# Long convolution and two MLPs on one core: operand blocks of a token pair as separate tasks, a spent input place turned into tiles, and weight sums streamed for both batches

## The chip, the cores and the metric

The kernel runs on one core of one Trainium2 chip. The metric is the device time of one execution in microseconds. Of the kernel before there are three timed runs (1117.55, 1117.56 and 1119.34 us) and one execution taken by the hardware profiler.

## The reference

Input `x` has 2 batches of 3008 tokens with 256 features. Three layers follow each other:

```
X = rfft(x, axis=1);  y = irfft(X * (filt_r + 1j*filt_i), n=3008, axis=1)    # long convolution along tokens
h = y @ w_in (256 x 2048);  g = max(h,0) + alpha*min(h,0);  z = g @ w_out (2048 x 256)      # first MLP, m = 0
h = max(z @ w_in2, 0);  out = (h*h) @ w_out2                                          # second MLP, m = 1
```

All is float32. The kernel keeps the precision by writing a float32 operand as a high half (rounded to the matmul's format) and a low half (what is left): a product is then three matmuls, high by high, high by low, low by high.

## The kernel before, in words

Features lie on the 128 partitions in two halves d = 0, 1, tokens along the free axis. `XS[b]` holds batch b's activations, 2 halves of 3008 tokens; each layer's result is written over its input there. The 3008 tokens of a batch are six tiles: four of 512 and two of 480 (`TILES`). The 2048 hidden features are 16 slices f of 128.

The work has these stages in time:

1. The convolution of batch 0, a four-step Fourier transform by matmuls (class `Conv`, `c0`).
2. The direct stage: the first MLP of batch 0, tile by tile (`h_mm`, `h_act`, `g_split`, `o_mm`). Beside it run the preparation of all weights (`weights`: halves made, written to DRAM as `WD`), the weight sums of MLP 1 (`sums`, written to DRAM as `SD`), and the beginning of batch 1's convolution (`c1`).
3. Nine token pairs, in this order: MLP 1 of batch 0, MLP 0 of batch 1, MLP 1 of batch 1, each with three pairs of tiles g = 0, 2, 4 (`pairs`, names (m, b, g)). In a pair the product of the input layer is done for two tiles and two feature slices at once with seven products in place of eight (Strassen's scheme in Winograd's form). One such step is a `square` (line 766); a pair has eight, c = 0 to 7, one for each two slices f. A square issues 7 products of 3 matmuls (line 801) and, in between, 8 waiting halves of the output layer (`o_half`, lines 636 to 638, 3 matmuls each). The rest of batch 1's convolution runs in the first three pairs (lines 306 to 308, 406).

For its seven products a pair needs seven operand blocks of the tokens: 11, 21, 22 (pieces of `XS`), and the differences T1 = 12 - 11, T2 = 22 - T1, T3 = 22 - 12, T4 = 21 - T2. `blocks` (line 663) makes them. Each takes a slot from `xb` (8 slots during the first three pairs, 11 later) for high and low half: ACT copies with rounding (line 694), then DVE subtracts for the low half (line 696). A difference is one DVE instruction (line 679) into a tile of `tf`. The squares use them in the order 11, 21, T2, T3, T1, 22, T4; a block's slot comes free after its last use in square 7 of its pair. In the kernel before, all seven blocks of a pair are one task, whose steps follow each other: a copy waits for the low half of the block before, and T3's and T4's differences come right before their copies.

For its products a square needs sums of weight blocks S1, S2, S3 (384 columns, high and low). For batch 0 they are loaded from `SD` into two `ring` tiles, two squares ahead (`fetch_sums`, line 532). For batch 1 six of the eight are loaded once per MLP into a place of their own, `sums`, which takes the place of `XS[0]`, and the last two into the ring.

`tf` (9 tiles of 512 columns, float32) holds intermediate values, and results on their way out (line 648); `tr` (9 tiles, rounded format) holds the halves of hidden activations.

The order is computed when the program is built. `Order` keeps a list of tasks (generators) and a time for each engine. Each step of a task names the engines it can run on with a cost, the events it needs and the tiles it takes. `run` picks the step that could begin earliest, less the task's `lead`, and issues it there; a tile is taken when the plan says it will be free. TensorE's own order is written out in the loops, and the other engines are filled up to a little ahead of it. On the chip every engine works off its queue in order, and waits where the plan was too early. SP issues all DMAs, in one queue.

Of the kernel before, what the change touches and what calls it, by code (L numbers as in the profile page):

```python
# [11 lines left out]
F32R = mybir.dt.float32r  # L12
# [6 lines left out]
B, S, D, FF = 2, 3008, 256, 2048  # L19
# [4 lines left out]
NF = FF // 128  # L24
TILES = [(i * 512, 512) for i in range(4)] + [(2048, 480), (2528, 480)]
# [7 lines left out]
N_TF = 9  # L33
# [8 lines left out]
PE_HOOK = 0.7  # L42
# [3 lines left out]
V2 = 4.8  # L46
# [9 lines left out]
ADD_V = 1.1  # L56
AHEAD = 2.5

LEAD0 = 0.3
LOWS, SUBS, LOWW = "VG", "VG", "VG"  # L60
LEAD1 = 0.5
GATE = ("SD", 1, 7)
SLACK = 0.6
LATE = ("WD", 1, 10)

TINY = 2.0 ** -15
INF = float("inf")
# [7 lines left out]
class Free:  # L75
# [5 lines left out]
    def when(self, n):  # L81
        return self.t[n - 1][0] if len(self.t) >= n + self.keep else None
# [19 lines left out]
HURRY = {}, [], []  # L102


class Spare:
# [5 lines left out]
    def when(self, n):  # L111
        t = self.free.t
        return t[n - 1][0] if len(t) >= n + self.keep else None


class Order:
# [76 lines left out]
def conv_mlp_mlp(ctx, tc, x, fil, wts, alp, cst, out):  # L193
    nc = tc.nc
    V, A, G, T, SP = nc.vector, nc.scalar, nc.gpsimd, nc.tensor, nc.sync
# [5 lines left out]
    def sb(name, cols, dt=F32, place=None):  # L201

        return pool.tile([128, cols], dt, name=name, tag=place or name)

    XS = [sb("X0", 2 * S), sb("X1", S + UC)]
# [3 lines left out]
    ring = [sb(f"ring{i}", 768, F32R) for i in range(2)]  # L209
    places = {f"stg{i}": sb(f"stg{i}", 1024) for i in range(N_STG)}  # L210
    stg = Free(places.values())
    tf = Free(sb(f"tf{i}", 512) for i in range(N_TF))
    tr = Free(sb(f"tr{i}", 512, F32R) for i in range(N_TR))
    xin = [sb(f"xin{i}", 2048) for i in range(NXS)]
    xs = Free([])
# [11 lines left out]


    SD = [[dram.tile([2, 128, 384], F32, name=f"s{m}_{c}") for c in range(NF // 2)] for m in range(2)]
    SX = []  # L230
    spare = Spare(tf, KEEP_S)
    wx = Free([])
    bf, br, wf, wr = Spare(tf, 0), Spare(tr, 0), Spare(tf, 0), Spare(tr, 0)
    xb = Free([])
# [7 lines left out]
    class Conv:  # L242
# [4 lines left out]
        def __init__(self, b, bank, whole, us, xin):  # L247
            self.b, self.bank, self.whole, self.us, self.xin = b, bank, whole, us, xin
            self.x, self.f = {}, {}
# [275 lines left out]
        mark(("SD", m, c), end)  # L525

    def sx(b, c, k):
        if b == 0 or c >= 6:
            return ring[c % 2][:, k * 384:k * 384 + 384]
        return SX[0][:, c * 768 + k * 384:c * 768 + k * 384 + 384]  # L530

    def fetch_sums(m, b, g, c, after):
        for k in range(2):
            _, end = yield {"S": 0.6}, [("SD", m, c), *after], []
            if b and c < 6 and not SX:
                SX.append(sb("sums", 768 * 6, F32R, "X0"))
            SP.dma_start(f32v(sx(b, c, k)), SD[m][c][k])
            end = od.moved(end, 128 * 1536)
        mark(("S", m, b, g, c), end)
# [123 lines left out]
    def blocks(m, b, g):  # L663

        o, n = TILES[g]
        need = [("Y", b, g), ("Y", b, g + 1)]
        if m == 0:
            need = [("X", 1, h, u) for h in range(2) for u in range(o // 376, (o + 2 * n - 1) // 376 + 1)]
        k = pairs.index((m, b, g))
        if k:  # L670
            need.append(("xb", *pairs[k - 1], "T4"))
        x = {f"{d + 1}{j + 1}": XS[b][:, d * S + o + j * n:d * S + o + j * n + n] for d in range(2) for j in range(2)}
        own = {}

        def less(name, p, q):
            _, end = yield {"V2": 0.69}, need, [(spare, 1)]
            own[name] = tf.take()
            x[name] = own[name][:, :n]
            V.tensor_sub(x[name], x[p], x[q])

        for name in ("11", "21", "T2", "T3", "T1", "22", "T4"):
            if name == "T2":
                yield from less("T1", "12", "11")
                yield from less("T2", "22", "T1")
            elif name == "T3":

                yield HURRY
                yield from less("T3", "22", "12")
            elif name == "T4":
                yield from less("T4", "21", "T2")  # L690
                tf.give(od.free["V"], own["T2"])
            _, end = yield {"A": 0.6}, need, [(xb, 1)]
            t = xb.take()
            A.copy(t[:, :n], x[name])  # L694
            _, end = yield {"V2": 0.69}, [], []
            V.tensor_sub(t[:, 512:512 + n], x[name], f32v(t[:, :n]))  # L696
            if name in own and name != "T2":
                tf.give(end, own[name])
            xsp[m, b, g, name] = t
            mark(("xb", m, b, g, name), end)  # L700

    oq = []
    pb = Free([])
# [62 lines left out]
    def square(m, b, g, c):  # L766

        n, f0, f1 = TILES[g][1], 2 * c, 2 * c + 1
        d0, d1 = slice(0, 128), slice(128, 256)
        w = {"11": (WH[f0][:, d0], WL[f0][:, d0]), "12": (WH[f0][:, d1], WL[f0][:, d1]), "22": (WH[f1][:, d1], WL[f1][:, d1])}  # L770
        w["S4"] = WH[f1][:, d0], WL[f1][:, d0]
        operands = {1: ("11", "11"), 2: ("12", "21"), 3: ("S4", "22"), 4: ("22", "T4"), 5: ("S1", "T1"), 6: ("S2", "T2"), 7: ("S3", "T3")}
        ps = {}
        od.add(chain(m, b, g, c, ps), joined(m, b, g, c, ps), lead=1.0)
        waits = {6: [("US", m, b, g, c, 1)], 5: [("US", m, b, g, c, 6)], 3: [("US", m, b, g, c, 5)], 4: [("J", m, b, g, c)]}
        for k in (1, 2, 0, 6, 0, 7, 5, 0, 0, 3, 0, 4, 0, 0, 0):
            if k:
                a, x = operands[k]
                need = [("xb", m, b, g, x), ("W", m, b, f0), ("W", m, b, f1), ("S", m, b, 0 if b else g, c)]
                if not all(e in at for e in need):  # L780
                    od.run(always, need)
                until = od.free["T"]
                after = waits.get(k, [])
                while not (all(e in at for e in after) if after else pb.t):
                    until += 0.5
                    od.run(dict.fromkeys(od.free, until))
                first = not after
                if first:
                    began = pb.t[0][0]
                    ps[k] = pb.take()  # L790
                else:
                    ps[k] = ps[7 if k == 4 else 1]
                    began = 0.0
                od.free["T"] = max(od.free["T"], began, *(at[e] for e in need + after)) + 3 * (n + 32) / 2400
                bank = ps[k]
                if a in ("S1", "S2", "S3"):
                    r = int(a[1]) * 128
                    w[a] = tuple(sx(b, c, j)[:, r - 128:r] for j in range(2))
                (wh, wl), t = w[a], xsp[m, b, g, x]
                for j, (p, r) in enumerate(((wh, t[:, :n]), (wh, t[:, 512:512 + n]), (wl, t[:, :n]))):  # L800
                    T.matmul(bank[:, :n], p, r, start=(first and j == 0), stop=(j == 2), skip_group_check=True)  # L801
                mark(("P", m, b, g, c, k), od.free["T"] + LATENCY)
                if c == NF // 2 - 1:
                    xb.give(od.free["T"], xsp.pop((m, b, g, x)))
            elif oq:
                ready, args = oq.pop(0)
                od.free["T"] = max(od.free["T"], ready)
                o_half(*args)
            ahead = od.free["T"] + AHEAD_S
            od.run({"A": ahead, "V": ahead, "G": ahead + 0.6, "S": od.free["T"] + 2.6, **({} if b else {"T": od.free["T"] + PE_HOOK})})  # L810
        mark(("done", m, b, g, c), od.free["T"])
# [21 lines left out]
    with tc.manual_schedule():  # L833
# [72 lines left out]

        od.add(reclaim([("O", 0, 0, t5 - 1, 2)], 2), *(reclaim_xs() for _ in range(NXS)), lead=1.0)
        od.add(reclaim([("SD", m, c) for m in range(2) for c in range(NF // 2)] + [("U", 1, u) for u in range(NU)], N_STG - 2))
        od.add(*(blocks(*k) for k in pairs), lead=0.9)
        whole = [("X", 1, h, g) for h in range(2) for g in range(8)]  # L910
        for m, b in ((1, 0), (0, 1), (1, 1)):
            for f in range(NF):
                after = [("O", 1 - m, b if m else 0, t, f) for t in (t5 - 1, t5)]
                od.add(fetch(m, b, f, after))
                if b and f % 2:
                    od.add(fetch_sums(m, b, 0, f // 2, after + whole + [("done", *pairs[2], f // 2), ("xb", *pairs[2], "T4")]))
        flat = [(g, c) for g in range(0, len(TILES), 2) for c in range(NF // 2)]
        for i, (g, c) in enumerate(flat):
            od.add(fetch_sums(1, 0, g, c, [("done", 1, 0, *flat[i - 2])] if i > 1 else [("O", 0, 0, t5, 4)]), lead=1.0)

        now = max(od.free["T"], at["xs", 0, 0, 0])
        for i in range(len(seq)):
# [18 lines left out]
        spare.keep = 2  # L941
        for k in pairs:
            if k == (0, 1, 0):
                od.run(always, whole)
                pb.give(od.free["T"], c0.bank.take(), c0.bank.take())
            for c in range(NF // 2):
                square(*k, c)
# [82 lines left out]
```

## Time and profile before

| | |
|---|---|
| timed runs, median of 3 | 1117.56 us |
| the profiled execution, its own time | 1120.31 us |
| its span in the profile | 1118.5 us |
| granted clock, mean | 0.996 |
| PE busy | 1103.3 us |
| DVE, ACT, POOL busy | 839.2, 742.0, 118.3 us |
| moved by DMA | 110.67 MB |

The span runs from the first to the last instruction of the profile. PE is TensorE's matmul row; matmuls overlap, so the time between two starts, not the length of one, is what a matmul costs. A bracket behind a row says how long the engine stood idle before it and which instruction released it.

### The profile page before, as it was taken

How to read it: one execution, taken by the hardware profiler on the slowest of the kernel's cores; microseconds unless marked ns; L12 is line 12 of the kernel's file. 1: busy time of each engine (PE TensorE's matmuls, PEld its weight loads, DVE VectorE, ACT ScalarE, POOL GpSimd, SP SyncE). 2: the span in 40 equal slices, each digit the busy share in tenths (PEclk: the TensorE clock that was granted, in tenths of full speed). 3: DMA queues.
4: the chain of work that ended last, by engine and by line, in shares of the span. 5: the costliest groups of instructions: out<-in, count | busy, mean ns of one | idle time of the engine just before them, and what ended most of it. 6: DMA issues, size and time to landing. Idle time of an engine off the chain costs nothing.

```text
span 1118.5 us, 14481 instructions
## 1 busy us (share of the span) xinstructions
PE 1103.3 (99%) x4945; PEld 907.3 (81%) x4946; DVE 839.2 (75%) x1361; ACT 742.0 (66%) x1360; POOL 118.3 (11%) x111
## 2 busy tenths in 40 slices
PE   9999999999999998999899999999999999999998
PEld 4678888888888887888698888888888888888887
DVE  4888878888889687769885887977977756656554
ACT  4777575665677676666566866766766666766665
POOL 5600000100022323313210000000000000000000
PEclk9999999999999999999999999999999999999999
DMA  9655223225746323223478700000144200100100
GB/s 232 173 199 197 80 90 125 90 88 163 234 132 214 125 70 109 85 71 90 123 245 259 228 1 1 1 1 1 37 140 151 88 1 1 38 1 1 39 1 36
DMA packets 64634, 110.67 MB, mean 99 GB/s; under 512 B 7472, under 2 KB 36400, under 8 KB 64560
## 3 DMA queue, kind: packets, MB, share of 16 engines
q1 hardware_dynamic: 64560, 109.74, 31.2%
q8 instruction: 39, 0.64, 0.2%
q14 instruction: 35, 0.29, 0.1%
HBM read 79.43 MB, written 30.28 MB: 98 GB/s over the span
## 4 chain that ended last, share of the span: by engine, by line
PE 96%; DVE 2%; ACT 1%; issue 0%; DMA 0%; ACTq 0%; DVEq 0%
PE bank L801 30%; PE bank L636 15%; PE bank L637 15%; PE bank L638 15%; PE bank L591 11%; PE bank L406 2%; PE bank L301 2%; PE bank L356 1%; PE bank L308 1%; PE bank L306 1%; PE bank L307 1%; PE bank L352 1%; PE bank L831 0%; DVE tr L622 0%; DVE xs L696 0%; PE bank L838 0%
## 5 line engine op out<-in xcount | busy, mean ns | idle before, releaser
L636 PE MATMUL bank<-tr,Wh 128*128 128x512 f32 (+1 forms) x768 | 300.3, 391 | 0.1
L638 PE MATMUL bank<-tr,Wh 128*128 128x512 f32 (+1 forms) x768 | 297.4, 387 | 0.0
L762 DVE TENSOR_TENSOR tr<-tf,tr 128x512 fp32r<-128x512 f32 (+1 forms) x288 | 193.3, 689 | 62.5 <-ACT tr L760 57.3
L711 ACT COPY tf<-bank 128x512 f32<-128x512 f32 (+1 forms) x216 | 124.8, 578 | 128.6 <-PE bank L801 128.5
L760 ACT CAST tr<-tf 128x512 fp32r<-128x512 f32 (+1 forms) x288 | 174.4, 612 | 22.3 <-DVE tf L757 12.2
L636 PEld LDWEIGHTS bank<-tr,Wh 128*128 128x128 f32 x768 | 144.7, 188 | 29.4 <-ACT tf L647 1.8
L638 PEld LDWEIGHTS bank<-tr,Wh 128*128 128x128 f32 x768 | 144.8, 189 | 28.1
L637 PE MATMUL bank<-tr,Wl_rest 128*128 128x512 f32 (+1 forms) x384 | 149.0, 388 | 0.0
L637 PE MATMUL bank<-tr,Wl 128*128 128x512 f32 (+1 forms) x384 | 148.7, 387 | 0.0
L724 DVE CUSTOM_DVE_ANT_0 tf<-bank,tf 128x512 f32<-128x512 f32 (+1 forms) x144 | 97.7, 679 | 60.7 <-PE bank L801 33.0
L755 ACT ACTIVATE tf<-tf 128x512 f32<-128x512 f32 (+1 forms) x147 | 91.5, 624 | 50.9 <-DVE tf L724 48.0
L801 PE MATMUL bank<-xs,Wh 128*128 128x512 f32 (+1 forms) x384 | 119.0, 390 | 5.2 <-ACT xs L694 2.7
L591 PE MATMUL bank<-xs,Wh 128*128 128x512 f32 (+1 forms) x384 | 118.0, 388 | 0.6 <-ACT X L398 0.6
L801 PEld LDWEIGHTS bank<-xs,Wh 128*128 128x128 f32 x384 | 71.3, 188 | 19.9 <-ACT xs L694 3.3
L604 ACT ACTIVATE tf<-bank 128x512 f32<-128x512 f32 (+1 forms) x96 | 56.6, 590 | 46.3 <-PE bank L591 46.0
L621 ACT CAST tr<-tf 128x512 fp32r<-128x512 f32 (+1 forms) x96 | 58.8, 612 | 42.9 <-DVE tf L605 42.3
L605 DVE SCALAR_TENSOR_TENSOR tf<-tf,one_minus_alpha,bank 128x512 f32<-128x512 f32 (+1 forms) x96 | 70.4, 734 | 22.2 <-ACT tf L604 21.7
L622 DVE TENSOR_TENSOR tr<-tf,tr 128x512 fp32r<-128x512 f32 (+1 forms) x96 | 68.6, 715 | 20.4 <-ACT tr L621 17.2
L637 PEld LDWEIGHTS bank<-tr,Wl_rest 128*128 128x128 f32 x384 | 72.5, 189 | 13.9
L637 PEld LDWEIGHTS bank<-tr,Wl 128*128 128x128 f32 x384 | 72.4, 189 | 12.7
L591 PEld LDWEIGHTS bank<-xs,Wh 128*128 128x128 f32 x384 | 71.2, 188 | 13.8 <-ACT X L398 0.8
L726 DVE TENSOR_TENSOR tf<-bank,tf 128x512 f32<-128x512 f32 (+1 forms) x72 | 48.9, 679 | 22.5 <-PE bank L801 12.6
(133 smaller groups left out, 1735.7 us busy)
## 6 DMA issues: line engine op xcount, KB each, us to landing
stg<-in_wts SPq DMA_DIRECT2D x30, 512.0 KB, 4.6
Wh<-w SPq DMA_DIRECT2D x48, 256.0 KB, 2.9
ring<-s SPq DMA_DIRECT2D x56, 192.0 KB, 3.8
Wl<-w SPq DMA_DIRECT2D x24, 256.0 KB, 3.6
Wl_rest<-w SPq DMA_DIRECT2D x24, 256.0 KB, 4.0
stg<-in_fil SPq DMA_DIRECT2D x16, 384.0 KB, 3.3
sums<-s SPq DMA_DIRECT2D x24, 192.0 KB, 3.9
w<-Wh SPq DMA_DIRECT2D x16, 256.0 KB, 2.2
```

The lines of the kernel that those rows point to most:

```text
L591: T.matmul(ps[:, :n], w, r, start=(j == 0), stop=(j == 5))
L605: V.scalar_tensor_tensor(p[:, :n], q[:, :n], oma[:, f:f + 1], ps, op0=ALU.mult, op1=ALU.add)
L622: V.tensor_sub(gl[:, :n], p[:, :n], f32v(gh[:, :n]))
L636: T.matmul(ps[:, :n], WH[f][:, w], gh[:, :n], start=(k == 0), stop=False)
L637: T.matmul(ps[:, :n], WL[f][:, w], gh[:, :n], start=False, stop=False)
L638: T.matmul(ps[:, :n], WH[f][:, w], gl[:, :n], start=False, stop=(k == NF - 1))
L711: A.copy(ps["u", k][:, q], ps[1][:, q])
L724: V._custom_dve(TENSOR_ADD_SAT, out=p[:, q], in0=ps[k][:, q], in1=ps["u", u][:, q], s0=INF, s1=0.0)
L755: A.activation(p[:, q], p[:, q], AF.Square)
L760: A.copy(h[:, q], p[:, q])
L762: V.tensor_sub(l[:, q], p[:, q], f32v(h[:, q]))
L801: T.matmul(bank[:, :n], p, r, start=(first and j == 0), stop=(j == 2), skip_group_check=True)
```

## The change

- `blocks` gives eight tasks in place of one. Task `early` makes the differences T3, T2 (now as T3 + 11) and T4: in the second and third pair of an MLP and batch once square 4 of the previous pair is issued, in the first one once block 21 has its slot. Each block has a task of its own; its turn comes when the block before has got its slot and its copy, and no longer when that block's low half is made. T1 is still made right before its copy. T3's tile is given back when T2 is made, T2's when T4 is made.
- The tasks' lead goes from 0.9 to 0.6, and the step that raised it to 1.0 in between (`HURRY`) goes.
- A new task `spent`: once the seven blocks of a pair of batch 0 are made, the pair's place in `XS[0]` is given to `tf` (four tiles for 512 tokens, two for 480), and for each two of them one of the nine original `tf` tiles is taken out and becomes a `tr` tile.
- The place `sums` goes; all weight sums of all nine pairs are loaded into the ring, each after the square two before it.
- `LEAD0` (the lead of what is left of the first stage, and of the weights of MLP 0, in the direct stage) goes from 0.3 to 1.0; `LATE` (when batch 1's convolution may begin to load) from the store of weight 10 of MLP 1 to that of weight 12.
- Before pair (0, 1, 0), halves of the output layer that wait are issued while batch 1's convolution isn't planned to its end.

```
-LEAD0 = 0.3
+LEAD0 = 1.0
-LATE = ("WD", 1, 10)
+LATE = ("WD", 1, 12)
...
     def sx(b, c, k):
-        if b == 0 or c >= 6:
-            return ring[c % 2][:, k * 384:k * 384 + 384]
-        return SX[0][:, c * 768 + k * 384:c * 768 + k * 384 + 384]
+        return ring[c % 2][:, k * 384:k * 384 + 384]
...
-        if k:
-            need.append(("xb", *pairs[k - 1], "T4"))
+        key = m, b, g
         x = {...}
+        names = "11", "21", "T2", "T3", "T1", "22", "T4"
...
+        def early():
+            gate = [("done", *pairs[k - 1], NF // 2 - 4)] if g else [("slot", *key, "21")]
+            for name, op, p, q in (("T3", "tensor_sub", "22", "12"), ("T2", "tensor_add", "T3", "11"), ("T4", "tensor_sub", "21", "T2")):
+                _, end = yield {"V2": 0.69}, [*need, *gate], [(spare, 1)]
+                own[name] = tf.take()
+                x[name] = own[name][:, :n]
+                getattr(V, op)(x[name], x[p], x[q])
+                mark(("own", *key, name), end)
+
+        def block(i, name):
+            turn = [("slot", *key, names[i - 1])] if i else [("slot", *pairs[k - 1], "T4")] if k else []
+            if name in ("T2", "T3", "T4"):
+                turn.append(("own", *key, name))
+            if name == "T1":
+                _, end = yield {"V2": 0.69}, [*need, *turn], [(spare, 1)]
+                own[name] = tf.take()
+                x[name] = own[name][:, :n]
+                V.tensor_sub(x[name], x["12"], x["11"])
+            yield {"A": 0.6}, [*need, *turn], [(xb, 1)]
             t = xb.take()
+            mark(("slot", *key, name), od.free["A"])
             A.copy(t[:, :n], x[name])
             _, end = yield {"V2": 0.69}, [], []
             V.tensor_sub(t[:, 512:512 + n], x[name], f32v(t[:, :n]))
-            if name in own and name != "T2":
+            if name in ("T1", "T4"):
                 tf.give(end, own[name])
+            elif name in ("T3", "T2"):
+                nxt = ("own", *key, "T2" if name == "T3" else "T4")
+                yield {}, [nxt], []
+                tf.give(max(end, at[nxt]), own[name])
...
-        od.add(*(blocks(*k) for k in pairs), lead=0.9)
+        od.add(*(task for k in pairs for task in blocks(*k)), lead=0.6)
...
-                if b and f % 2:
-                    od.add(fetch_sums(m, b, 0, f // 2, after + whole + [("done", *pairs[2], f // 2), ("xb", *pairs[2], "T4")]))
-        flat = [(g, c) for g in range(0, len(TILES), 2) for c in range(NF // 2)]
-        for i, (g, c) in enumerate(flat):
-            od.add(fetch_sums(1, 0, g, c, [("done", 1, 0, *flat[i - 2])] if i > 1 else [("O", 0, 0, t5, 4)]), lead=1.0)
+        flat = [(*k, c) for k in pairs for c in range(NF // 2)]
+        for i, k in enumerate(flat):
+            od.add(fetch_sums(*k, [("done", *flat[i - 2])] if i > 1 else [("O", 0, 0, t5, 4)]), lead=1.0)
+
+        def spent(g):
+            _, end = yield {}, [("xb", 1, 0, g, k) for k in ("11", "21", "T2", "T3", "T1", "22", "T4")], []
+            o, n = TILES[g]
+            t = [XS[0][:, d * S + o + j * 512:d * S + o + j * 512 + 512] for d in range(2) for j in range(2 if n == 512 else 1)]
+            tf.give(end, *t)
+            for _ in range(len(t) // 2):
+                yield {}, [], [(old, 1)]
+                at_, t = old.entry()
+                tf.t.remove((at_, t))
+                k = next(k for k, v in homes.items() if v is t)
+                tr.give(at_, sb(f"tr_{k}", 512, F32R, k))
+
+        od.add(*(spent(g) for g in range(0, len(TILES), 2)), lead=1.0)
...
             if k == (0, 1, 0):
+                while oq and not all(e in at for e in whole):
+                    ready, args = oq.pop(0)
+                    od.free["T"] = max(od.free["T"], ready)
+                    o_half(*args)
+                    od.run(dict.fromkeys(od.free, od.free["T"] + PE_HOOK))
                 od.run(always, whole)
```

## Rows read from the trace of the kernel before

**Rows 1.** The page: PE's busy time, and the chain that ended last.

```profile
PE 1103.3 (99%) x4945; PEld 907.3 (81%) x4946; DVE 839.2 (75%) x1361; ACT 742.0 (66%) x1360; POOL 118.3 (11%) x111
...
PE 96%; DVE 2%; ACT 1%; issue 0%; DMA 0%; ACTq 0%; DVEq 0%
```

**Rows 2.** Busy us (x count) by stretch, PE, PEld, DVE, ACT, POOL; clock, DMA share, GB/s.

```profile
416.00:436.00 20.00, 17.11 (x66) 12.76 (x65) 15.82 (x26) 12.88 (x25) 8.76 (x8) 0.91 0.38 120
...
526.00:550.00 24.00, 20.16 (x78) 15.12 (x77) 21.19 (x32) 13.17 (x25) 5.79 (x5) 0.93 0.29 100
...
632.00:714.00 82.00, 81.94 (x360) 67.09 (x359) 67.04 (x104) 56.93 (x100) 0.00 (x0) 1.00 0.11 35
```

**Rows 3.** PE's waits: for whom, us in total, times, longest.

```profile
PE bank L801 <- DVE xs L696: 3.5, 3, 1.7
PE bank L801 <- ACT xs L694: 2.7, 2, 2.3
PE bank L591 <- DVE Wl L456: 1.3, 1, 1.3
```

**Rows 4.** PE's instructions at 430: start, us, instruction, [idle before, releaser].

```profile
430.11 0.49 PE L801 MATMUL bank<-xs,Wh 128*128 128x512 f32 x1 [2.31 <-ACT xs L694]
430.83 0.50 PE L801 MATMUL bank<-xs,Wh 128*128 128x512 f32 x1 [0.23 <-DVE xs L696]
...
431.49 0.63 PE L636 MATMUL bank<-tr,Wh 128*128 128x512 f32 x1
431.91 0.63 PE L637 MATMUL bank<-tr,Wl_rest 128*128 128x512 f32 x1
```

**Rows 5.** The chain that ended last, 425 to 431: start, us, what.

```profile
425.67 3.02 DMA out<-tf
...
428.71 0.70 DVE tf L679
...
429.44 0.63 ACT xs L694
...
430.09 0.70 DVE xs L696
```

**Rows 6.** PE's instructions at 536 and 545.

```profile
536.09 0.70 PE L801 MATMUL bank<-xs,ring 128*128 128x480 f32 x2 [1.68 <-DVE xs L696]
...
545.30 0.48 PE L801 MATMUL bank<-xs,Wh 128*128 128x480 f32 x1 [1.61 <-DVE xs L696]
```

**Rows 7.** The chain that ended last, 531 to 545.

```profile
531.61 1.39 DVE tf L679
...
534.66 1.39 DVE xs L696
...
543.00 1.69 DVE tf L757
```

**Rows 8.** Line 679: count, ns min/median/max, first and last start, forms.

```profile
L679 DVE TENSOR_TENSOR tf<-X x18: 649/684/1464, 248.0 to 958.2; 128x512 f32<-128x512 f32 x12, 128x480 f32<-128x480 f32 x6
```

**Rows 9.** POOL's instructions at 534.

```profile
534.36 1.17 POOL L292 TENSOR_TENSOR tr<-tf,tr 128x384 fp32r<-128x384 f32 x1 [1.87 <-ACT tr L290]
```

**Rows 10.** Line 537, the loads of weight sums: issues (ns), and us to landing.

```profile
L537 SPq DMA_DIRECT2D ring<-s x56: 320/383/1670, 275.8 to 879.5; - x56
...
L537 SPq DMA_DIRECT2D sums<-s x24: 320/430/1030, 588.3 to 858.3; - x24
...
DMA to landing us min/median/max: 2.3/3.8/6.3
```

**Rows 11.** SP's queue: batch 1's first load, the store of weight 12.

```profile
291.48 0.37 SPq L254 DMA_DIRECT2D stg<-in_x  x1
...
311.81 1.05 SPq L466 DMA_DIRECT2D w<-X  x2
```

**Rows 12.** Batch 1's convolution: lines 377 (last transposition) and 406 (last products).

```profile
L377 DVE STREAM_TRANSPOSE X<-bank x24: 669/710/720, 36.1 to 561.7; 128x512 f32<-128x512 f32 x24
...
L406 PE MATMUL bank<-cst,X x192: 242/281/327, 54.6 to 589.1; 128*128 128x94 f32 x192
```

More of the change, by code (lines that the diff above doesn't have):

```diff
@@ L113, in when, with __init__, entry @@
         return t[n - 1][0] if len(t) >= n + self.keep else None
+class Among:
+    def __init__(self, free, tiles):
+        self.free, self.tiles = free, tiles
+    def entry(self):
+        return next((e for e in self.free.t if any(e[1] is k for k in self.tiles)), None)
+    def when(self, n):
+        e = self.entry()
+        return e[0] if e else None
 class Order:
@@ L211, in conv_mlp_mlp @@
     stg = Free(places.values())
-    tf = Free(sb(f"tf{i}", 512) for i in range(N_TF))
+    homes = {f"tf{i}": sb(f"tf{i}", 512) for i in range(N_TF)}
+    tf = Free(homes.values())
+    old = Among(tf, homes.values())
     tr = Free(sb(f"tr{i}", 512, F32R) for i in range(N_TR))
@@ L229, in conv_mlp_mlp @@
     SD = [[dram.tile([2, 128, 384], F32, name=f"s{m}_{c}") for c in range(NF // 2)] for m in range(2)]
-    SX = []
     spare = Spare(tf, KEEP_S)
@@ L534, in fetch_sums @@
             _, end = yield {"S": 0.6}, [("SD", m, c), *after], []
-            if b and c < 6 and not SX:
-                SX.append(sb("sums", 768 * 6, F32R, "X0"))
             SP.dma_start(f32v(sx(b, c, k)), SD[m][c][k])
@@ L669, in blocks @@
         k = pairs.index((m, b, g))
-        if k:
-            need.append(("xb", *pairs[k - 1], "T4"))
+        key = m, b, g
         x = {f"{d + 1}{j + 1}": XS[b][:, d * S + o + j * n:d * S + o + j * n + n] for d in range(2) for j in range(2)}
+        names = "11", "21", "T2", "T3", "T1", "22", "T4"
         own = {}
[L675 to L692, printed above, removed]
+        def early():
[16 more added lines that the diff above has]
+            yield {"A": 0.6}, [*need, *turn], [(xb, 1)]
             t = xb.take()
+            mark(("slot", *key, name), od.free["A"])
             A.copy(t[:, :n], x[name])
@@ L696, in blocks @@
             V.tensor_sub(t[:, 512:512 + n], x[name], f32v(t[:, :n]))
-            if name in own and name != "T2":
+            if name in ("T1", "T4"):
                 tf.give(end, own[name])
+            elif name in ("T3", "T2"):
+                nxt = ("own", *key, "T2" if name == "T3" else "T4")
+                yield {}, [nxt], []
+                tf.give(max(end, at[nxt]), own[name])
             xsp[m, b, g, name] = t
             mark(("xb", m, b, g, name), end)
+        return [early(), *(block(i, name) for i, name in enumerate(names))]
     oq = []
@@ L778, in square @@
                 a, x = operands[k]
-                need = [("xb", m, b, g, x), ("W", m, b, f0), ("W", m, b, f1), ("S", m, b, 0 if b else g, c)]
+                need = [("xb", m, b, g, x), ("W", m, b, f0), ("W", m, b, f1), ("S", m, b, g, c)]
                 if not all(e in at for e in need):
```

## The prediction

> **What bounds the kernel now.** I read the page's busy shares first. PE is busy 1103.3 us, 99% of the span [rows 1]; the other engines have room. The chain that ended last agrees: 96% of it is PE [rows 1]. So only two things can move the end: fewer or shorter matmuls, or the few microseconds in which PE stands. The change leaves every matmul as it is (same products, same widths), so I looked only for PE's standing time.
>
> The busy shares by stretch show where it is [rows 2]. A later pair, 632 to 714, does 360 matmuls in 82.00 us, 0.228 us each; that is the undisturbed rate. The stretch 416 to 436 has 66 matmuls in 20 us, where 88 would fit, and 526 to 550 has 78 in 24 us, where 105 would. In both the granted clock is below one (0.91 and 0.93). Each holds the passage from one token pair to the next: (1,0,0) to (1,0,2) near 418, (1,0,2) to (1,0,4) near 528. By count these two passages lose (88-66)*0.228 = 5.0 us and (105-78)*0.228 = 6.2 us, together 11.2 us.
>
> The wait list says on what [rows 3]: PE at L801 waits for the two halves of an operand block, ACT's copy (L694) and DVE's low half (L696). The next is 1.3 us, once, for a weight's low half.
>
> PE's timeline gives the same loss from the rows [rows 4, 6]. First passage: idle 2.31 and 0.23 us, and from 431.5 on matmuls come 0.43 us apart instead of 0.23 [rows 4], so the level is 1.2 instead of 2.4 GHz. With a clock of 0.91 over 20 us, at 0.5 while it is low, this lasted 0.09*20/0.5 = 3.6 us and cost half of that, 1.8 us. Sum 4.3 us. Second passage: idle 1.68 and 1.61 us among the rows shown, and 0.07*24/0.5 = 3.4 us at the low level, cost 1.7 us [rows 2, 6]. Sum 5.0 us. Together 9.3 us by rows against 11.2 us by count; I take 10.2 us, halfway, for the two passages.
>
> **The change, part by part.**
>
> *Differences early, blocks as tasks.* The chain through the first passage [rows 5] reads: an out-transfer holds a tf tile for 3.02 us, DVE's difference L679 (this is T4 = 21 - T2) takes the tile at 428.71, ACT copies it at 429.44, DVE makes the low half at 430.09, and PE goes on at 430.83. So the last operand was begun only when a tile came free, and its serial chain of about 2.1 us followed. The second passage [rows 7] is the same chain with DVE as its limit: the difference T3 at 531.61 (1.39 us on the path), low halves at 534.66 (1.39), and later two instructions of L757 (1.69) ahead of the last low half. In the new code T3, T2 and T4 are made when three squares of the previous pair are still to do, some 31 us ahead (a square is 82/8 = 10.2 us by [rows 2], more where the transform shares PE); T4's difference then stands neither behind the out-transfer nor at the passage. T1 stays just in time. The block tasks hand on their turn at ACT's copy and no longer at DVE's low half, so ACT's next copy need not stand behind it. Instructions: four differences a pair as before, 36 in all in the trace (18 of one form [rows 8] and as many of the other); one subtraction became an addition of the same operand kind. DVE's total does not move.
>
> What is late next: T1's difference, its copy and its low half, and the order of freed block slots (still 8 until the conv and the sums are done). Each passage can so give back all its 5.1 us or nothing. The nearest row for what stays is the fourth pair, whose first 82 us hold no shortfall in the count [rows 2]; but it had all block slots and no transform beside it. I let 1.0 us stand in each passage: gain 10.2 - 2.0 = 8.2 us, ends 0 and 10.2.
>
> *The Trainium skill on this.* The trace shows DVE's two-input instructions stretched where POOL works: L679 has a median of 684 ns and a maximum of 1464 [rows 8], and the POOL instruction of 534.36 [rows 9] lies beside the low half that took 1.39 us. The Trainium skill, "GPSIMD Engine Reference", section 1 (Specifications), says that GpSimd's SBUF interface is shared with VectorE and that instructions with two SBUF inputs contend for it. The trace agrees with it. It speaks against this change in so far as the early differences, and the low halves that stay at the passage, are all of that kind: the second passage would keep its stretched instructions. That is rival C below, and its price is from rows.
>
> *Spent token places as tiles.* After a pair's seven blocks are made, its four 512-wide pieces of batch 0's place (two for 480) become tf tiles, and half as many old tf tiles become tr tiles: 9 and 9 grow to 11 and 11 in the first pair, 13 and 13 in the second, 14 and 14 in the third. It issues no instruction. It pays back the three tiles that the early differences hold for some 31 us. Where it comes too late, those tiles are missing; that is rival D. Within the later pairs PE shows no loss that more tiles could lift [rows 2], so I add nothing: 0, bounds 0 and a gain of 1.
>
> *Weight sums streamed for batch 1.* The resident place for six of eight sum tiles goes. Before, 24 loads into it and 8 of the 56 ring loads served batch 1; now 6 pairs of 8 squares with two loads each, 96, so 64 loads of 192 KB more [rows 10]. At 0.38 us of issue each this is 24 us on SP, spread over about 490 us; the DMA share of the first of these pairs is 0.11 [rows 2]. A ring tile is asked for when the square two before it is done and needed about one square later: 10.2 us for a landing of 3.8, at most 6.3 [rows 10]. Behind the waiting issue on SP stand out-transfers and weight loads, which need later products anyway. Batch 0 ran so for 24 squares, and PE's waits name no ring [rows 3]. Cost 0; if the cover were gone, a landing that is 6.3 - 3.8 = 2.5 us late once a pair would cost 6 * 2.5 = 15 us, the far bound; the nearest row says 0.
>
> *Leads and gate.* A larger lead of the tasks left over from the transform (0.3 to 1.0) puts the weights' work ahead of other tasks of the direct stage. What it can lift is the wait of 1.3 us for Wl [rows 3]; I take 1.0 us, bounds 1.3 and a loss of as much. The later gate for batch 1's transform moves its first load from 291.48 past the store of weight 12 at 311.81 [rows 11], 20 us. Its cover: the transform's last product is at 589.1 [rows 12], 43 us before pair (0,1,0) needs it near 632. With 8 us of stalls gone PE arrives sooner, so 43 - 20 - 8 = 15 us remain. Cost 0. The new loop that runs waiting halves when the transform is not ready changes nothing while that cover holds.
>
> Sum: 8.2 + 1.0 = 9.2 us less. The profiled execution took 1120.31 us (its span 1118.5 and 1.8 around it), 2.8 above the median 1117.56 of the runs shown; the stalls are in PE's order and should be in every run, so the difference goes off the median: 1117.56 - 9.2 = 1108.4, I say 1108.
>
> **The rivals.**
> B, the change moves the stalls and does not lift them: the tiles are again late, at another block. For it: the order is planned ahead with fixed costs (0.69 us for a difference), while the trace has 649 to 1464 ns for it [rows 8]. Against: the rows name one tile and one serial chain. Time 1117.5.
> C, one passage stays: POOL's instructions beside the second passage keep DVE's low halves at 1.39 us, and its 5.1 us remain. For: [rows 7, 9]. Against: the T3 difference in that chain goes. Time 1117.56 - 9.2 + 4.1 = 1112.5 (1.0 of the 5.1 was left in already).
> D, slower: the early differences hold three of 11 tf tiles in the first pair, and the gate starts batch 1's transform 20 us later; the transform falls behind by more than the 15 us of cover left. The price is its serial rest with PE waiting for it: from the last unit's transposition to the last product it is 561.7 to 589.1, 27 us [rows 12], of which the halves still queued can fill some. If half is exposed, 14 us: 1117.56 - 9.2 + 14 = 1122. It decides once the transform's last product comes later than the end of the third pair. Against it: tiles grow as soon as the first pair's blocks are made.
>
> **How the numbers follow.** The forecast (both passages mostly lifted) 0.52, with a range of its own of 1104 to 1111; C 0.22; B 0.10; D 0.16. About 0.2% (2.2 us) is what a measurement of this kernel tells from no change. Forecast and C are faster: 0.74; B is the same: 0.10; D is slower: 0.16. Range: the low end is full recovery by the higher count, 11.2 + 1.3 and 1 for tiles, 1117.56 - 13.5 = 1104.1, and half a microsecond below it: 1103.5. The high end takes in B and D's lighter half: 1119.5. Outside are some 0.12 above and 0.05 below.
>
> **What would show it.** Right: in the busy shares by stretch the passages to the second and third pair run at 0.228 us a matmul with a clock of 1.00; PE's wait list loses most of its 6.2 us for L694 and L696; difference rows lie well before the passage; the sums' ring has over 140 loads and PE waits on none. The end of the last pair moves to about 1105 in the span. Wrong: new waits of PE at L801 for a ring load or a block in the batch 1 pairs; the transform's last product later than the third pair's end, with PE idle near 620; or the same two dips in the clock.

## The result and the profile after

| | before | after |
|---|---|---|
| median | 1118.24 us (4 runs) | 1107.78 us (4 runs, 1107.68 to 1108.13) |
| ratio after to before | | 0.9906, 95% interval [0.9889, 0.9923] |
| profiled execution, its span | 1120.31, 1118.5 us | 1107.81, 1106.0 us |

The change makes the kernel 0.94% faster, 10.5 us by the medians and 12.5 us between the two profiled executions. The forecast was 1108.0 us, and the case that came is the one it held likeliest. Its sum, though, was right for only part of the reasons it gave, as the experiments show.

The page of the kernel after, PE's busy time and the chain that ended last, to be read beside [rows 1]:

```profile
PE 1097.1 (99%) x4945; PEld 905.3 (82%) x4946; DVE 839.3 (76%) x1344; ACT 741.5 (67%) x1362; POOL 139.0 (13%) x126
...
PE 97%; DVE 2%; issue 1%; ACT 0%; DVEq 0%; ACTq 0%
```

PE has the same 4945 matmuls and DVE the same busy time. Busy time by stretch of the kernel after, columns as in [rows 2]; the first two rows lie where the first and second passage now are:

```profile
416.00:436.00 20.00, 19.07 (x85) 15.20 (x84) 18.75 (x29) 15.30 (x29) 7.36 (x7) 1.00 0.41 132
...
516.00:540.00 24.00, 23.83 (x109) 19.84 (x108) 22.39 (x36) 16.01 (x32) 6.59 (x5) 1.00 0.37 116
...
622.00:704.00 82.00, 82.00 (x362) 67.65 (x361) 65.43 (x101) 56.45 (x98) 0.00 (x0) 1.00 0.19 61
```

Where 66 matmuls stood in 20 us there are 85, where 78 stood in 24 us there are 109, and the granted clock is 1.00 in both. The later pair is as it was. To see where the gain lies, take the first products of the first and of the fourth pair, before and then after:

```profile
325.84 0.61 PE L801 MATMUL bank<-xs,Wh 128*128 128x512 f32 x2
...
625.00 0.63 PE L801 MATMUL bank<-xs,Wh 128*128 128x512 f32 x2
```

```profile
324.50 0.61 PE L822 MATMUL bank<-xs,Wh 128*128 128x512 f32 x2
...
612.99 0.61 PE L822 MATMUL bank<-xs,Wh 128*128 128x512 f32 x2
```

The first three pairs took 299.2 us and take 288.5 us: 10.7 of the 12.5 us between the two profiled executions lie in them, and 1.3 us ahead of them. The last 442 us of each kernel's span, before and after:

```profile
676.00:1118.00 442.00, 438.55 (x1956) 365.88 (x1955) 299.53 (x467) 291.68 (x515) 0.00 (x0) 1.00 0.10 34
```

```profile
664.00:1106.00 442.00, 437.43 (x1955) 365.93 (x1953) 304.57 (x474) 291.73 (x514) 0.00 (x0) 1.00 0.20 63
```

1956 and 1955 matmuls: the tail is the same to one matmul, though the DMA share doubled (0.10 and 0.20). The whole list of PE's waits after, beside [rows 3] (the first group is the start of the kernel):

```profile
PE bank L859 <- DVE zeros L856: 1.2, 1, 1.2
PE bank L321 <- DVE X L380: 0.9, 1, 0.9
PE bank L602 <- DVE Wl_rest L471: 0.8, 1, 0.8
PE bank L602 <- ACT X L413: 0.6, 1, 0.6
PE bank L822 <- DVE tf L745: 0.4, 2, 0.3
PE bank L421 <- DVE X L392: 0.3, 1, 0.3
```

No operand block is in it any more (they are lines 709 and 711 now); the experiments show that this holds for this order of instructions and not for each of its neighbours. Of the direct stage, the wait of 1.3 us for Wl is gone, and that for Wl_rest went from 0.3 to 0.8 us.

The differences of the second pair, DVE's instructions of line 693 after the change, and below them T1's difference (705) and low halves (711) at the passage:

```profile
380.48 1.50 DVE L693 TENSOR_TENSOR tf<-X 128x512 f32<-128x512 f32 x1
383.15 0.65 DVE L693 TENSOR_TENSOR tf<-tf,X 128x512 f32<-128x512 f32 x1
385.60 1.18 DVE L693 TENSOR_TENSOR X<-X,tf 128x512 f32<-128x512 f32 x1
...
413.48 1.51 DVE L705 TENSOR_TENSOR X<-X 128x512 f32<-128x512 f32 x1
...
422.36 1.51 DVE L711 TENSOR_TENSOR xs<-X,xs 128x512 fp32r<-128x512 f32 x1
```

T4's difference is done at 386.8, some 30 us ahead of the passage; before, it stood at 428.71 in the middle of it [rows 5]. It writes into a tile named X, one of the pieces of batch 0's place. The stretched DVE instructions are still there: POOL has one from 413.40 to 414.44, beside T1's difference of 1.51 us. In this execution they cost nothing, since no wait of PE names them.

### The profile page after: what moved, and what is told of

Its sections match the earlier page's. It is cut to its first block, busy times and chain, and to the rows that moved or that the text cites. A ratio compares the mean times of both kernels' runs of the same rounds, so it can differ in the third digit from the quotient of the medians.

```text
span 1106.0 us, 14459 instructions
## 1 busy us (share of the span) xinstructions
PE 1097.1 (99%) x4945; PEld 905.3 (82%) x4946; DVE 839.3 (76%) x1344; ACT 741.5 (67%) x1362; POOL 139.0 (13%) x126
## 4 chain that ended last, share of the span: by engine, by line
PE 97%; DVE 2%; issue 1%; ACT 0%; DVEq 0%; ACTq 0%
PE bank L822 30%; PE bank L647 15%; PE bank L649 15%; PE bank L648 15%; PE bank L602 12%; PE bank L421 2%; PE bank L316 2%; PE bank L371 1%; PE bank L321 1%; PE bank L323 1%; PE bank L322 1%; PE bank L367 1%; DVE xs L711 1%; PE bank L852 0%; DVE tf L745 0%
## 5 line engine op out<-in xcount | busy, mean ns | idle before, releaser
L647 PE MATMUL bank<-tr,Wh 128*128 128x512 f32 (+1 forms) x650 | 252.8, 389 | 0.1
L649 PE MATMUL bank<-tr,Wh 128*128 128x512 f32 (+1 forms) x498 | 192.5, 386 | 0.0
L732 ACT COPY X<-bank 128x512 f32<-128x512 f32 (+1 forms) x154 | 88.8, 577 | 88.5 <-PE bank L822 87.8
L647 PEld LDWEIGHTS bank<-tr,Wh 128*128 128x128 f32 x650 | 122.0, 188 | 25.0 <-ACT X L658 1.1
L649 PEld LDWEIGHTS bank<-tr,Wh 128*128 128x128 f32 x498 | 93.5, 188 | 18.1
L649 PE MATMUL bank<-tr_tf,Wh 128*128 128x512 f32 (+1 forms) x270 | 104.1, 386 | 0.0
L781 ACT CAST tr<-X 128x512 fp32r<-128x512 f32 (+1 forms) x150 | 91.5, 612 | 10.2 <-DVE X L778 4.5
L822 PE MATMUL bank<-xs,ring 128*128 128x480 f32 (+1 forms) x336 | 88.9, 384 | 0.0
L822 PE MATMUL bank<-blocks_stg,ring 128*128 128x512 f32 (+1 forms) x312 | 86.3, 391 | 0.0
L633 DVE TENSOR_TENSOR tr<-tf,tr 128x512 fp32r<-128x512 f32 (+1 forms) x96 | 68.3, 712 | 23.4 <-ACT tr L632 20.1
L632 ACT CAST tr<-tf 128x512 fp32r<-128x512 f32 (+1 forms) x96 | 58.7, 612 | 39.4 <-DVE tf L616 39.2
L822 PEld LDWEIGHTS bank<-xs,ring 128*128 128x128 f32 x336 | 62.7, 188 | 11.2 <-DVE X L745 0.2
```

What stands on the lines that cost most here:

```text
L632: A.copy(gh[:, :n], p[:, :n])
L633: V.tensor_sub(gl[:, :n], p[:, :n], f32v(gh[:, :n]))
L647: T.matmul(ps[:, :n], WH[f][:, w], gh[:, :n], start=(k == 0), stop=False)
L649: T.matmul(ps[:, :n], WH[f][:, w], gl[:, :n], start=False, stop=(k == NF - 1))
L732: A.copy(ps["u", k][:, q], ps[1][:, q])
L781: A.copy(h[:, q], p[:, q])
```

## The experiments

Theory T: the differences made early and the block tasks lift the passages. Rival S: the added tiles do. Rival L: the leads do. A fourth reading, R, came up on the way: much of 1107.8 is the luck of one order. All twelve kernels were timed against the kernel before; each ratio is to that kernel, with its 95% interval in brackets. The changed kernel has 0.9906.

**No tiles (e1).** The changed kernel without the tasks that give the spent place away.

```diff
-        od.add(*(spent(g) for g in range(0, len(TILES), 2)), lead=1.0)
```

> The changed kernel without the tasks that turn batch 0's spent place into tiles; tf and tr stay at 9 and 9. Theory T (the differences made early and the block tasks lift the two passages): within 2 us of the changed kernel's 1107.8, both passages at full clock. Theory S (the added tiles lift them, since the old chain waited for a tf tile): back to 1114 or more, with PE waiting at one or both passages. Should the three held tiles starve the convolution of batch 1 (the forecast's rival D), its last product comes later than 600 us and the time goes over 1118.

Measured: 1121.84 us, ratio 1.0019 [1.0010, 1.0028], slower than before. The first passage is lifted even so: PE's waits name no block there, and 414 to 434 has 90 matmuls at a clock of 1.00. The second is not: the wait of 1.9 us below, at 526.18, is for the last block's low half there. And PE now stands elsewhere too. PE's waits, and the last products of batch 1's transform (line 421), in e1:

```profile
PE bank L421 <- ACT X L413: 3.8, 3, 1.7
PE bank L822 <- DVE xs L711: 1.9, 1, 1.9
```

```profile
L421 PE MATMUL bank<-cst,X x192: 242/281/524, 54.6 to 625.6; 128*128 128x94 f32 x192
```

The same line in the changed kernel:

```profile
L421 PE MATMUL bank<-cst,X x192: 242/281/355, 54.3 to 577.7; 128*128 128x94 f32 x192
```

The transform ends 48 us later than with the tiles. The stretch 520 to 620 of e1, and the same of the changed kernel:

```profile
520.00:620.00 100.00, 95.33 (x450) 81.84 (x448) 79.42 (x146) 65.34 (x127) 28.72 (x23) 0.98 0.52 164
```

```profile
520.00:620.00 100.00, 99.83 (x489) 86.58 (x488) 78.10 (x143) 72.52 (x144) 14.93 (x12) 1.00 0.63 199
```

39 matmuls fewer, at 0.228 us some 9 us, of which the second passage has a part. PE waits for the transform's last copies, and what is left of the transform runs with nothing beside it, at a granted clock of 0.68 over 615 to 626:

```profile
615.86 0.71 PE L421 MATMUL bank<-cst,X 128*128 128x94 f32 x4 [0.43 <-ACT X L413]
618.27 1.44 PE L421 MATMUL bank<-cst,X 128*128 128x94 f32 x8 [1.71 <-ACT X L413]
621.42 4.58 PE L421 MATMUL bank<-cst,X 128*128 128x94 f32 x20 [1.71 <-ACT X L413]
```

This is the forecast's rival D in its mechanism. That its 1122 fits to 0.2 us is in part luck: some of the loss stands at the second passage, and the fourth pair too takes 83.7 in place of 81.8 us. Both theories get half: the early differences lift the first passage without the tiles, and lose more than that without them.

**Old blocks (e2).** The changed kernel with the old serial block task, lead 0.9.

```diff
-        od.add(*(task for k in pairs for task in blocks(*k)), lead=0.6)
+        od.add(*(blocks(*k) for k in pairs), lead=0.9)     # and blocks() as before
```

> The changed kernel with the old block task: one serial task a pair, differences right before their copies, lead 0.9; tiles, streaming and leads stay changed. Theory T: the passages stall again, 1114 to 1118, with PE waiting on L694/L696-type copies and low halves for over 4 us. Theory S: within 2 us of 1107.8, since tiles are there in time for the differences.

Measured: 1118.28 us, 0.9992 [0.9982, 1.0002], no gain. PE's timeline at the first passage of e2 (copy and low half are lines 705 and 707 there, L722 and L735 the sums' copies and additions):

```profile
428.86 0.50 PE L812 MATMUL bank<-xs,Wh 128*128 128x512 f32 x1 [0.32 <-DVE xs L707]
431.54 0.50 PE L812 MATMUL bank<-xs,Wh 128*128 128x512 f32 x1 [1.25 <-ACT xs L705]
432.27 0.50 PE L812 MATMUL bank<-xs,Wh 128*128 128x512 f32 x1 [0.23 <-DVE xs L707]
```

The chain there, start, us, what:

```profile
428.84 0.69 DVE tf L735
429.53 1.32 DVE tf L690
...
430.87 0.63 ACT xs L705
...
431.52 0.70 DVE xs L707
```

The tile is there in time (no out-transfer in this chain, unlike [rows 5]), but T4's difference (L690, stretched to 1.32 us) still stands right ahead of its copy, behind DVE's other work. So S alone falls: tiles without the new blocks give nothing. That is theory T's expectation (PE's waits for blocks are 4.7 us in all, the time 0.3 us above its range). In the nine variants that keep the new block tasks these waits are 0 to 2.4 us in all; in the kernel before they are 6.5 us, and in the two other variants with the old task, e4 and e7, 6.3 and 7.0.

**Old leads (e3), leads alone (e4).**

```diff
-LEAD0 = 1.0
-LATE = ("WD", 1, 12)
+LEAD0 = 0.3
+LATE = ("WD", 1, 10)
```

> The changed kernel with LEAD0 back at 0.3 and LATE back at the store of weight 10. Theory T and theory S alike: 1107.8 to 1110, the wait for Wl of about 1.3 us back in the direct stage. Theory L (the leads carried a good part of the gain by keeping the convolution out of the weights' way): 1111 or more.

> The kernel before with LEAD0 at 1.0 and LATE at the store of weight 12 as its only changes. If the leads are worth by themselves what their removal cost in the changed kernel (5 to 6 us): 1112 to 1114. If they pay only together with the new blocks and tiles: 1117 to 1119, both passages still stalling; the weight wait of 1.3 us in the direct stage goes in either case.

Measured: e3 (this edit on the changed kernel) 1113.58 us, 0.9942 [0.9923, 0.9961]; e4 (the reverse on the kernel before) 1118.87 us, 0.9998 [0.9988, 1.0007]. By themselves the leads give nothing, and both passages still stall. In the changed kernel their absence costs 4 us by ratio, which looked like theory L, until the neutral edits below cost as much. In e3 the wait of 1.3 us for Wl is back and in e4 it is gone, both as expected; in e4 that for Wl_rest went from 0.3 to 0.8 us, and a new one of 1.3 us stands in the convolution of batch 0.

**Not early (e5), turn after the low half (e6).**

```diff
-            gate = [("done", *pairs[k - 1], NF // 2 - 4)] if g else [("slot", *key, "21")]
+                gate = ("slot", *key, "22" if name == "T4" else "21")
```

```diff
-            turn = [("slot", *key, names[i - 1])] if i else [("slot", *pairs[k - 1], "T4")] if k else []
+            turn = [("xb", *key, names[i - 1])] if i else [("xb", *pairs[k - 1], "T4")] if k else []
```

> The changed kernel with each difference made at its own block's turn (T3 and T2 once block 21 has its slot, T4 once block 22 has its slot), the blocks still tasks of their own and T2 still T3 + 11. If making them early is what counts within theory T: 1111 to 1116, with a difference row right ahead of PE's wait at a passage. If the tasks' overlap (turn handed on at the copy) or the tiles are enough: within 2 us of 1107.8.

> The changed kernel with the turn handed on at the end of the low half, as in the old task, in place of the copy; differences still early. If the overlap of copy and low half counts within a passage: 1110 to 1115, PE waiting at a passage on a copy that follows a low half. If making the differences early is what counts: within 2 us of 1107.8.

Measured: e5 1114.65 us, 0.9954 [0.9939, 0.9968]; e6 1111.34 us, 0.9930 [0.9915, 0.9945]. Neither falls back to the kernel before. In e5 PE's waits in the first three pairs name no block at all; the four longest groups of six:

```profile
PE bank L822 <- ACT X L732: 1.5, 2, 1.0
PE bank L322 <- DVE tr L307: 1.5, 1, 1.5
PE bank L822 <- ACT tf L732: 1.0, 1, 1.0
PE bank L649 <- DVE tr L783: 0.6, 2, 0.3
```

They are at sums' copies (732), the transform (307) and hidden halves (783). So "a difference right ahead of PE's wait" was a miss. In e6 a wait of 1.1 us for a block's low half stands at the first passage, as the overlap would have it, but the time is that of the neutral edits below.

**Streaming alone (e7), and doubled (e8, e9).** e7 is the kernel before with all sums streamed. In e8 each ring load is issued twice and the plan counts both; in e9 the plan counts one, and PE, DVE, ACT and POOL have the order of the changed kernel.

```diff
             SP.dma_start(f32v(sx(b, c, k)), SD[m][c][k])
+            SP.dma_start(f32v(sx(b, c, k)), SD[m][c][k])
             end = od.moved(end, 128 * 1536)
+            end = od.moved(end, 128 * 1536)     # e8 only
```

> The kernel before with all weight sums streamed through the ring and nothing else changed (no tiles, old blocks, old leads). The forecast says streaming costs nothing: 1117 to 1120, as before, no wait of PE on the ring. Should 64 more loads on SP's queue cost (the far bound of the forecast): up to 1133, with PE waiting for ring loads in the batch 1 pairs.

> The changed kernel with every ring load issued twice, the same data into the same place, so 288 loads in place of 144. If the ring has the cover that the forecast gives it (10.2 us for a landing of about 3): within 2 us of 1107.8. If the queue or the landing is near its limit: PE waits at L822 on the ring and the time rises by 2.5 us or more for each pair, to 1120 or more.

> The changed kernel with every ring load issued twice, and the second one hidden from the plan, so that the order of PE, DVE, ACT and POOL is that of the changed kernel and SP alone has 144 loads more. Theory of free streaming: 1107.5 to 1109, no wait of PE on the ring. If the loss seen with the planned double loads (1113) came from the loads themselves and not from another order: 1111 to 1115.

Measured: e7 1119.75 us, 1.0008 [0.9997, 1.0020], the same as before, as expected. e8 1113.02 us, 0.9944 [0.9928, 0.9961], with no wait of PE on the ring. e9 1141.62 us, 1.0227 [1.0198, 1.0255], which no theory had. SP's own waits in e9 say why:

```profile
SPq L548 <- DMA ring<-s: 339.9, 144, 6.1
SPq L548 <- PE bank L822: 149.0, 45, 8.2
```

Each second load waits in SP's queue until the first has landed, 144 times, 340 us together, and everything behind it on SP waits too. The chain that ended last shows it at one place, 361 to 379: the ring holds SP, a load of batch 1's transform is issued only then, and ACT's copy of a sum (732), behind the transform's work on ACT, comes late; PE stands 5.0 us until 378.95.

```profile
361.17 5.15 DMA ring<-s
...
366.80 2.42 DMA ring<-s
...
371.14 6.58 DMA stg<-in_x
...
378.41 0.48 ACT X L732
```

But look at where the waits cost time. The last 442 us of e9, to set beside the two rows shown above:

```profile
696.00:1138.00 442.00, 438.84 (x1961) 367.14 (x1959) 305.95 (x476) 292.66 (x516) 0.00 (x0) 1.00 0.32 101
```

1961 matmuls against 1955: from the later part of the fourth pair on, even doubled loads with their waits cost nothing. The stretch leaves out the first 53 us of that pair, which is a batch 1 pair, and there they do cost. PE's waits of e9 in 642 to 800:

```profile
PE bank L822 <- DMA ring<-s: 2.7, 2, 2.1
```

The fourth pair takes 85.5 us in e9 (first product to that of the fifth) and 81.8 in the changed kernel; two more such waits, 3.4 us, stand in the third pair. So "no wait of PE on the ring" was missed under doubled loads. The rest of the loss lies ahead of the fourth pair, where transform loads stand behind the ring in SP's queue, as in the chain above; how much of it each such load makes was not taken apart. So e9 was no pure test of the loads, as its expectation took it to be; for the last five pairs it is a strong one.

**Neutral edits (e10, e11, e12).** Three edits of the changed kernel too small to be meant for anything.

```diff
-LEAD0 = 1.0
+LEAD0 = 0.9                          # e10
-LATE = ("WD", 1, 12)
+LATE = ("WD", 1, 11)                 # e11
-... for task in blocks(*k)), lead=0.6)
+... for task in blocks(*k)), lead=0.7)      # e12
```

> The changed kernel with LEAD0 at 0.9 in place of 1.0, a change too small to be meant for anything. If the changed kernel's 1107.8 is what its parts give to any order (theory T with the tiles): within 2 us of it. If a good part of it is the luck of one order (theory R), as the 3 to 6 us suggest that every edit of a part has cost so far: 1110 to 1115, with a stall of 2 us or more at some other place of the first three pairs.

> The changed kernel with the gate of batch 1's transform at weight 11 in place of 12. Parts theory: within 2 us of 1107.8. Theory R (luck of the order): 1110 to 1115, stalls elsewhere in the first three pairs.

> The changed kernel with the block tasks' lead at 0.7 in place of 0.6. Parts theory: within 2 us of 1107.8. Theory R: 1110 to 1115, stalls elsewhere in the first three pairs.

Measured: 1112.10 us, 0.9944 [0.9929, 0.9959]; 1112.45 us, 0.9945 [0.9930, 0.9960]; 1110.99 us, 0.9936 [0.9921, 0.9951]. All three are 3 to 5 us above the changed kernel, as R expected. The waits of PE between 320 and 625 in e12:

```profile
PE bank L822 <- DVE tf L745: 2.8, 2, 2.6
PE bank L321 <- DVE X L380: 0.9, 1, 0.9
```

The changed kernel has the same two groups there, with 0.4 and 0.9 us (its list is shown above). One wait of 2.6 us at an addition (745) is new. R's "elsewhere" did not come in e12: the wait stands at 536.51, at the second passage itself. Between 415 and 560, e10 and then e11 wait for operand blocks again:

```profile
PE bank L822 <- DVE blocks_stg L711: 0.7, 1, 0.7
```

```profile
PE bank L822 <- DVE xs L711: 1.9, 2, 1.4
```

So how far the passages are lifted hangs on the order too: in all three neighbours a part of a stall is back at one of them or both, beside waits at other places in e10 and e11. In e10 no single wait reaches the 2 us that R expected; the longest are 1.4 us. An edit that only shuffles the order costs 0.30 to 0.39% here. Against this, e4 (0.9998 where the kernel before has 1) and, beside the changed kernel, e3 (0.9942), e6 (0.9930) and e8 (0.9944) show nothing of their own, and e5 (0.9954) is 0.09 to 0.18% above the neutral ones with overlapping intervals: what the leads, the handing on of the turn and the early time are worth each was not settled. Clear of this scatter are e1 (no tiles), e2 (old blocks) and the kernel before.

None of the variants beat the changed kernel.

## Why the prediction was right, and where it was not

- *What bounds the kernel*: right. 10.7 of the 12.5 us between the profiled executions are gained in the three pairs that hold the two passages, and nothing in the last 442 us moved.
- *Size of the passages*: 10.2 us taken as lost, 2.0 left in, 8.2 gained. By the same count as [rows 2], after has 85 where 88 fit and 109 where 105 fit (480 columns, and some of the transform's products, are shorter), so under 1 us is left; the three pairs' 10.7 us say the same. What was let stand was too much by some 1 us each in this order; in e11 waits of 0.5 and 1.4 us for a block stay at the two passages, about what was let stand.
- *Which part lifts them*: half right. The working gave all of it to early differences and block tasks, and 0 (at most 1) to the tiles. That term failed, as the gain needs both: with the old blocks (e2) nothing is gained, and without the tiles the same kernel takes 1121.84 us, 14 us more by the medians and 12.6 by the ratios. It was the forecast's own rival D that told what the tiles prevent, and priced it at 1122; it was not carried over into the tiles' term, because the later pairs showed no loss that more tiles could lift. The place to look was the transform's tiles in the first three pairs: its last product comes at 603.5 in e4 (new leads and gate alone), at 625.6 in e1 (all but the tiles), and at 560.3 in e2 (all but the new blocks).
- *The gate's cover*: 43 - 20 - 8 = 15 us expected. Two of these terms were off: the fourth pair's first product came at 625.00 and not near 632, so the cover before was 36 us, and the transform's first load moved by 38 us, from 291.48 to 329.3. By the same sum 36 - 38 - 8 leaves none. Yet its last product came earlier, 577.7 against 589.1 [rows 12], and 35 us are left before the fourth pair's first product at 612.99. The tiles, which had 0 in the sum, made up for the gate: with them the transform runs faster than it was delayed, without them it comes at 625.6.
- *Leads, 1.0 us*: not shown. The wait of 1.3 us for Wl went and that for Wl_rest grew by 0.5 us. The first pair began 1.3 us earlier, but in e4, with the same leads, 1.5 us later than before (at 327.3), and e4 has no gain.
- *Streaming, 0*: right, by e7 and, from the fifth pair on, by e9. What it is for is the place: `sums` took `XS[0]`, which `spent` now gives to `tf`.
- *Contention with POOL (the Trainium skill, "GPSIMD Engine Reference", section 1)*: the trace agrees that two-input DVE instructions stretch beside POOL, 1.50 and 1.51 us against a median of 0.68. Over the whole execution after, none of the 344 of them (128x512, both inputs in SBUF) with no POOL instruction beside took over 0.70 us, and the 35 with more than 0.3 us of one beside have a median of 1.18. Rival C, that this would keep the second passage, did not come: PE waits for none of the stretched instructions.
- *The median*: the difference of 9.2 us was taken off 1117.56; the four runs of before have 1118.24, and the difference was 10.5. A start 0.7 us too low and a gain 1.3 us too small cancelled in part, so that 1108 lies closer to 1107.78 than its terms do: that is luck. And by the neutral edits some 3 to 4 us of the 10.5 belong to this one order, which the forecast had no term for: its 9.2 us lie between the neighbours' gains (6 to 7 us) and the measured one.

## What to carry to other kernels

Where an engine is 99% busy, count its instructions in equal stretches and look for the few stretches that hold fewer; the wait list of those alone says what to move. Starting work early holds its buffers longer: price the buffers as a part of the change, since here the early start without more tiles was slower than before, and both together gave 0.94%. In a kernel whose order is planned as a whole, time two or three neutral edits before a small gain is put down to a part; here three of them moved the time by 0.3 to 0.4%, all upward.

## What was not expected of the hardware

The kernel before varies from run to run more than the one after, as far as four executions of the latter can tell: its executions lie between 1116.80 (clock 1.000 over the span) and 1121.32 us, while those after lie within 0.45 us at 0.999 or 1.000. In the main the time goes with the clock: of 45 executions of the kernel before, in the experiments, the four at 1.000 took 1116.80 to 1117.63 us, the 27 at 0.998 1117.60 to 1120.03, the four at 0.997 1119.17 to 1121.32, and the ten at 0.996 1119.96 to 1120.96.

The dips of the clock to the 1.2 GHz level in [rows 2, 4] follow idle stretches of PE of 2.31 and 1.68 us, and do not come in every execution of the same program; the wait of 1.61 us [rows 6] was not followed by one. The length of the wait alone does not tell. In e2 a dip follows the waits of 1.25 and 0.23 us shown above, and in e8 none follows one of 2.12 us, at 540.12. The stretches of e2 and of e8:

```profile
431.00:438.00 7.00, 6.23 (x19) 4.73 (x20) 4.80 (x8) 4.90 (x10) 0.00 (x0) 0.76 0.39 132
```

```profile
538.00:546.00 8.00, 5.88 (x33) 5.29 (x33) 6.44 (x14) 5.78 (x14) 2.28 (x2) 1.00 0.75 244
```

So a passage that stalls costs its idle time and, in some runs, up to 1.8 us more by the estimate of the prediction. That this explains the whole spread was not tried.
